# Block-recurrent attention and quick-GELU MLP: the states' exponentials are turned by DMA and VectorE, not by TensorE

## The chip, the cores and the metric

The kernel runs on one core of a Trainium2 chip. The metric is the device time of one execution in microseconds (us), as a median of several executions. The profile reports the span from the first to the last instruction; the device time is about 1.8 us longer in most runs. All runs quoted are of the undisturbed ("fast") state.

## The reference

```python
# x (8, 8, 512, 64), state (8, 8, 32, 64), float32; scale = 1/8
a  = softmax(scale * x @ state.T)            # over the 32 states
xread = a @ state                            # 512 rows a batch
a2 = exp(scores2 - scores2.max(-1))          # scores2 = scale * state @ x.T, over 512 tokens
a2 /= a2.sum(-1) + 1e-9
sread = a2 @ x                               # 32 rows a batch
h = concat(xread, sread) @ w_in              # (4352, 512) @ (512, 2048)
out = (h * sigmoid(1.702 * h)) @ w_out
```

The change concerns `a2`, called `e2` in the kernel, and `sread`. The scores are small (inputs of standard deviation 0.1), so `a2` is nearly uniform. Some experiments below put wrong blocks into it on purpose, and the comparison with the reference passed for them too. "Correct" therefore says little about the addresses of the new transfers; for the versions recommended here I also compared the addresses with those of the change by hand.

## The kernel before

One batch's up and down products run on TensorE (PE) while the attention of the next batch is woven in. Names such as P5, P6, P3 and P7 are the partial products of a two-level Strassen scheme, in that order; each has seven small products, and a *hook* like "P3.5" is the place in program order after the fifth of them, where work of the next batch is put. Reading the states for batch b needs `e2` with tokens on the partitions, `eT`.

```python
def att_s_exp(b, room=None):                       # cut
    room = apool.tile([P, NPR, S], FP32, tag="xT", name=f"e2_{b}")
    for g in range(NG):                            # NG = 2
        nc.scalar.activation(out=room[:, g], in_=a["s"][g], func=AF.Exp, bias=..., scale=scale, accum_out=sm)

def s_norm(b, g):
    ...                                            # sm = 1 / (sm + eps), on VectorE
    nc.scalar.activation(out=e, in_=e, func=AF.Copy, scale=sm)          # batches 2 to 7

def att_eT(b, g):                                  # at hook "P6"
    ps = att_ps([P, SCH, P], f"eT_{b}_{g}")
    for c in range(SCH):                           # SCH = 4
        nc.tensor.transpose(ps[:, c], a["e2"][g][0][:, P * c : P * (c + 1)], ident)
    nc.scalar.copy(a["eT"][:, g], ps)

def att_sread(b):                                  # 64 small matmuls
    nc.tensor.matmul(ps[st, g], a["eT"][:, g, c, st], xn[b][:, c, NG * j + g], ...)
    nc.scalar.copy(sr, ps)

# strassen_two, after P6 (cut)
if plain:                                          # while batch 2's attention is woven in
    for fn in steps3: fn()                         # four big differences on VectorE
    hook("P6")
    product(bank(3), A_of(0, 1), B22, "P3")        # att_sread(2) at hook "P3a", halfway
else:                                              # batches 3 to 7
    low_load(3, 0)                                 # ahead of it, after P5: low_load(6, 1)
    hook("P6")
    lowly("P3", left12, B22, low_b, ...)           # low_b: what low_load(6, 1) brings, 768 KB
    hook("run")                                    # att_sread(b)
```

The second small product of P3, called P3.2 below, is the first that reads `low_b`. Its load can only be issued at the end of P5, which read other sums from the same buffer.

## Time and profile before

| | before |
|---|---|
| time | 720.39 us, median of 3 (720.36 to 720.54) |
| span of the profiled run | 718.7 us |
| PE busy, share of the span | 704.6 us, 98% |
| VectorE (DVE) busy | 586.4 us, 82% |
| ScalarE (ACT) busy | 241.6 us, 34% |
| DMA queue, share of 16 engines | 104304 packets, 32.6% |

The shares say that PE is the bound and that DVE is the next candidate; the rest of the reading is in the prediction. One more view matters later, the table of PE's waits. Each line has the waiting line, what it waited for, the total in us, how often, and the longest. The largest before is 1.5 us, at 36 us, before the batches that are changed; no line is for a load of the low sums that P3.2 reads.

### The profile page before, as it was taken

The page shows a single profiled execution, that of the slowest core. Times are in us where ns is not written, and L with a number is a line of the kernel's source. Part 1 is how long each engine was busy: PE and PEld are TensorE (multiplying, and loading weights), DVE is VectorE, ACT ScalarE, POOL GpSimd, SP SyncE. Part 2 cuts the span into 40 slices and gives each one's busy share as a digit, 9 for nine tenths or more (in the row PEclk, how much of TensorE's full clock was granted, in tenths as well). Part 3 has the DMA queues.
Part 4 walks back from the last instruction along what each step waited for, and adds up shares of the span by engine and source line. Part 5 has one row for each costly group of instructions (what it writes and reads, how often), then busy time and mean ns, then how long its engine had stood idle before and what let it go on. Part 6 is the DMA issues. An engine that isn't in the chain of part 4 may idle for free.

```text
span 718.7 us, 12329 instructions
## 1 busy us (share of the span) xinstructions
PE 704.6 (98%) x4949; PEld 561.7 (78%) x4951; DVE 586.4 (82%) x1199; ACT 241.6 (34%) x467; POOL 0.8 (0%) x8
## 2 busy tenths in 40 slices
PE   8989999999999999999999999999999999999996
PEld 3433444467898799879998899889987998899995
DVE  6998899739868998699878986899789987989440
ACT  5686511024214422524233423342244215200210
POOL 0000000000000000000000000000000000000000
PEclk9999999999999999999999999999999999999999
DMA  9921246016153334405450445133422340031001
GB/s 234 357 87 58 91 147 145 6 59 160 47 175 63 58 106 162 77 1 123 158 121 0 110 142 133 18 74 125 154 50 51 112 162 15 1 117 61 17 1 29
DMA packets 104361, 68.43 MB, mean 95 GB/s; under 512 B 87664, under 2 KB 95344, under 8 KB 104304
## 3 DMA queue, kind: packets, MB, share of 16 engines
q1 hardware_dynamic: 104304, 67.65, 32.6%
q8 instruction: 39, 0.64, 0.4%
q14 instruction: 18, 0.15, 0.1%
HBM read 54.79 MB, written 12.85 MB: 94 GB/s over the span
## 4 chain that ended last, share of the span: by engine, by line
PE 88%; DVE 5%; DMA 3%; ACT 2%; SPq 1%; issue 1%; DVEq 0%; ACTq 0%
PE low L669 17%; PE o L1064 17%; PE o L720 14%; PE o L669 8%; PE o L518 7%; PE h L500 7%; PE upx L1064 6%; PE M L320 4%; PE o L561 2%; DMA xn<-in_x_dram 2%; PE o L320 1%; PE sr L480 1%; PE warm L125 1%; DMA out_dram<-osb_sr 1%; PE eT L469 1%; DMA out_dram<-osb 1%
## 5 line engine op out<-in xcount | busy, mean ns | idle before, releaser
L1074 DVE TENSOR_TENSOR g<-o,g 128x512 f32<-128x512 f32 (+1 forms) x140 | 88.0, 650 | 55.5 <-PE o L1064 54.6
L720 PE MATMUL o<-w_out,g 128*128 128x256 f32 x480 | 107.9, 381 | 0.0
L720 PEld LDWEIGHTS o<-w_out,g 128*128 128x128 f32 x480 | 90.2, 190 | 18.3 <-issue 6.3
L1071 ACT ACTIVATE g<-g 128x512 f32<-128x512 f32 (+1 forms) x84 | 49.8, 600 | 101.9 <-DVE g L1074 101.9
L1064 PE MATMUL upx<-aT,M 128*128 128x256 f32 x192 | 49.3, 379 | 0.0
L1064 PE MATMUL o<-ta,M 128*128 128x256 f32 x192 | 49.3, 379 | 0.0
L1064 PE MATMUL o<-ta,ms 128*128 128x256 f32 x192 | 48.3, 379 | 0.0
L460 ACT COPY M<-M 128x512 f32<-128x512 f32 x64 | 33.2, 597 | 29.6 <-PE M L320 29.6
L1064 PEld LDWEIGHTS o<-ta,ms 128*128 128x128 f32 x192 | 36.5, 190 | 4.9
L1064 PEld LDWEIGHTS o<-ta,M 128*128 128x128 f32 x192 | 36.5, 190 | 4.9
L669 PE MATMUL low<-low,g 128*128 128x128 f32 x304 | 40.2, 275 | 0.0
L1064 PEld LDWEIGHTS upx<-aT,M 128*128 128x128 f32 x192 | 36.1, 190 | 4.7
L669 PEld LDWEIGHTS low<-low,g 128*128 128x128 f32 x304 | 37.0, 192 | 0.0
L669 PE MATMUL low<-sums,later 128*128 128x128 f32 x264 | 35.0, 276 | 0.1
L669 PEld LDWEIGHTS low<-sums,later 128*128 128x128 f32 x264 | 32.7, 192 | 0.7 <-DVE pu L674 0.3
L320 PE MATMUL M<-w_in,stT 64*32 64x512 f32 x512 | 32.6, 594 | 0.2 <-ACT eT L470 0.2
L541 DVE TENSOR_TENSOR later<-g,g 128x512 f32<-128x512 f32 (+1 forms) x32 | 20.8, 648 | 14.7 <-ACT g L503 14.7
L500 PE MATMUL h<-low,M 128*128 128x512 f32 x64 | 29.8, 600 | 1.5 <-DVE low L408 1.5
L500 PE MATMUL h<-aT,M 128*128 128x512 f32 x64 | 28.7, 599 | 1.4 <-ACT M L460 1.4
L518 PE MATMUL o<-w_out,g 128*128 128x512 f32 x64 | 28.7, 594 | 0.0
L669 PE MATMUL low<-w_out,g 128*128 128x128 f32 x216 | 28.5, 275 | 0.0
L518 PE MATMUL o<-w_out,sums 128*128 128x512 f32 x64 | 28.4, 594 | 0.0
(214 smaller groups left out, 1287.1 us busy)
## 6 DMA issues: line engine op xcount, KB each, us to landing
low<-low SPq DMA_DIRECT2D x34, 768.0 KB
later<-in_moe_w_out_dram SPq DMA_DIRECT2D x16, 512.0 KB
xn<-in_x_dram SPq DMA_DIRECT2D x28, 256.0 KB
w_out<-in_moe_w_in_dram SPq DMA_DIRECT2D x12, 512.0 KB
xsq<-in_x_dram SPq DMA_DIRECT2D x96, 64.0 KB
out_dram<-osb SPq DMA_DIRECT2D x18, 256.0 KB
out_dram<-later SPq DMA_DIRECT2D x14, 256.0 KB
later<-in_moe_w_in_dram SPq DMA_DIRECT2D x4, 512.0 KB
```

What stands on the lines that cost most here:

```text
L125: nc.tensor.matmul(ps, zeros[:, :P], zeros, start=True, stop=True)
L320: nc.tensor.matmul(ps[g][st], A[b]["stT"][rows, st], rhs(rows, j), start=True, stop=True)
L460: nc.scalar.copy(m[:, g], ps[g])
L500: nc.tensor.matmul(hps, lhs[i], rhs[i], start=(i == 0), stop=(i == n - 1))
L518: nc.tensor.matmul(ops, G[key, f // 2][:, f % 2, P * r : P * (r + 1)], w_out[:, f], start=(f == 0), stop=(f == NF - 1))
L541: nc.vector.tensor_tensor(out=s1, in0=a21, in1=a22, op=ALU.add)
L561: nc.tensor.matmul(ps[:, r], lhs[f][:, P * r : P * (r + 1)], rhs[:, f], start=(first and r == 0 and f == 0), stop=(f == HF - 1), skip_grou ...
L669: nc.tensor.matmul(ps, lhs[f], rhs[:, f], start=(first and f == 0), stop=(f == QF - 1), skip_group_check=True)
L720: nc.tensor.matmul(ps[:, r], lhs[f][:, P * r : P * (r + 1)], rhs[:, f], start=(r == 0 and f == 0), stop=(f == HF - 1), skip_group_check=True,)
L1064: nc.tensor.matmul(ps[:, k], lhs[i][:, o : o + P], rhs[i], start=(first and k == 0 and i == 0), stop=(i == n - 1), skip_group_check=True,)
L1071: nc.scalar.activation(out=dst, in_=src, func=AF.Gelu_apprx_sigmoid)
L1074: nc.vector.tensor_tensor(out=dst, in0=ps, in1=x, op=ALU.add)
```

## The change

For batches 2 to 7 the 8 transposes on PE and their 2 evictions on ACT go. Instead the exponentials are stored to DRAM, loaded back so that each 32x32 block sits at its transposed place, and each block is turned by DVE where it lies. The division by the sums moves from the exponentials to the result of the reads. Room on DVE is made by moving `x_scale` and `x_back` to earlier hooks.

```diff
+    squares = dram.tile([Ns, NG * NB, NPR, Ns], FP32, name="squares")
+    def eT_out(b):                                  # 4 stores of 128 KB, runs of 128 bytes
+        for j in range(NPR):
+            src = e2_room[b][Ns * j : Ns * (j + 1), :NG].rearrange("n g (t a) -> n (g t) a", a=Ns)
+            nc.sync.dma_start(squares[:, :, j], src)
+    def eT_in(b):                                   # 4 loads of 128 KB, runs of 512 bytes
+        v = squares.rearrange("n (k i) j a -> i n k (j a)", i=SCH)
+        for i in range(SCH):
+            nc.sync.dma_start(a["eT"][Ns * i : Ns * (i + 1)].rearrange("n g c q -> n (g c) q"), v[i])
+    def eT_turn(b, g):
+        t = A[b]["eT"][:, g].rearrange("p c q -> p (c q)")
+        nc.vector.transpose(t, t)
 # s_norm, batches 2 to 7
-            nc.scalar.activation(out=e, in_=e, func=AF.Copy, scale=sm)
 # att_sread, batches 2 to 7
-        nc.scalar.copy(sr, ps.rearrange("p g d -> p (g d)"))
+            for g in range(NG):
+                nc.scalar.activation(out=sr[:, D * g : D * (g + 1)], in_=ps[:, g], func=AF.Copy, scale=a["e2"][g][1])
 # hooks
+        at("P2a", eT_out, b)                        # after the exponentials
+        ("P5", eT_in)                               # behind low_load(6, 1)
-            ("P6", att_eT, 0), ("P6", att_eT, 1),
 # batches 3 to 7
-                ("P3.3", x_scale, 1), ("P3.4", x_back, 0), ("P3.5", x_back, 1)
+                ("P6.6", x_scale, 1), ("P3.3", x_back, 0), ("P3.4", x_back, 1), ("P3.5", eT_turn, 0), ("P3.6", eT_turn, 1)
 # batch 2
-                ("P6.5", x_scale, 1), ("P6.6", x_back, 0), ("P6", x_back, 1)
+                ("P6.5", x_scale, 1), ("P6.6", x_back, 0), ("P6", x_back, 1), ("P6", eT_turn, 0), ("P6", eT_turn, 1)
```

More of the change, by code (lines that the diff above doesn't have):

```diff
@@ L360, in att_s_max @@
             a["mx2"].append(mx)
+    e2_room = {}
     def att_s_exp(b, room=None):
@@ L364, in att_s_exp @@
         if room is None:
-            room = apool.tile([P, NPR, S], FP32, tag="xT", name=f"e2_{b}")
+            room = e2_room[b] = apool.tile([P, NPR, S], FP32, tag="xT", name=f"e2_{b}")
         a["e2"] = []
@@ L379, in s_norm @@
             nc.vector.tensor_scalar(e, e, sm, None, ALU.mult)
-        else:
-            nc.scalar.activation(out=e, in_=e, func=AF.Copy, scale=sm)
     def att_s_norm(b):
@@ L460, in att_M @@
             nc.scalar.copy(m[:, g], ps[g])
+    squares = dram.tile([Ns, NG * NB, NPR, Ns], FP32, name="squares")
[4 more added lines that the diff above has]
+    def eT_in(b):
+        a = A[b]
+        a["eT"] = apool.tile([P, NG, SCH, P], FP32, tag="eT", name=f"eT_{b}")
+        v = squares.rearrange("n (k i) j a -> i n k (j a)", i=SCH)
[4 more added lines that the diff above has]
+        nc.vector.transpose(t, t)
     def att_eT(b, g):
@@ L484, in att_sread @@
         sr = apool.tile([P, P], FP32, tag="sr", name=f"sr_{b}")
-        nc.scalar.copy(sr, ps.rearrange("p g d -> p (g d)"))
+        if b < 2:
+            nc.scalar.copy(sr, ps.rearrange("p g d -> p (g d)"))
+        else:
+            for g in range(NG):
+                nc.scalar.activation(out=sr[:, D * g : D * (g + 1)], in_=ps[:, g], func=AF.Copy, scale=a["e2"][g][1])
         A[b]["sr"] = sr
@@ L792, in strassen_two @@
             product(p5, [S1[:, f, :half] for f in range(HF)], T1, "P5")
+            hook("P5")
             banks = [h0, h1, o]
@@ L803, in strassen_two @@
             low_load(6, 1)
+            hook("P5")
             o, h0, h1 = low_banks()
@@ L932, in hooks_next @@
         attention = [
-            ("P6.1", x_sum, 0), ("P6.3", x_sum, 1), ("P6.3", x_inverse), ("P6.4", x_scale, 0), ("P6", att_eT, 0), ("P6", att_eT, 1),
+            ("P6.1", x_sum, 0), ("P6.3", x_sum, 1), ("P6.3", x_inverse), ("P6.4", x_scale, 0),
         ]
         if b > 2:
-            attention += [("P3.3", x_scale, 1), ("P3.4", x_back, 0), ("P3.5", x_back, 1)]
+            attention += [("P6.6", x_scale, 1), ("P3.3", x_back, 0), ("P3.4", x_back, 1), ("P3.5", eT_turn, 0), ("P3.6", eT_turn, 1)]
             names = {"T": range(5), "P7.5": (5, 6), "P7.6": (7,), "P4.1": (8,), "P4.5": (12, 13)}
@@ L939, in hooks_next @@
         else:
-            attention += [("P6.5", x_scale, 1), ("P6.6", x_back, 0), ("P6", x_back, 1)]
+            attention += [("P6.5", x_scale, 1), ("P6.6", x_back, 0), ("P6", x_back, 1), ("P6", eT_turn, 0), ("P6", eT_turn, 1)]
             names = {"P3a": range(7), "P7.1": (7,), "P7.2": (8,), "P7.3": (12, 13)}
             run, turned = "P3a", "P3b"
-        attention += [(run, att_sread), (run, att_M, 3, True), (run, att_M, 2)]
+        attention += [("P5", eT_in), (run, att_sread), (run, att_M, 3, True), (run, att_M, 2)]
         for name, fn, *args in attention:
```

## The prediction

> **What bounds the kernel now.** I read the page's busy shares and chain first.
>
> ```profile
> PE 704.6 (98%) x4949; PEld 561.7 (78%) x4951; DVE 586.4 (82%) x1199; ACT 241.6 (34%) x467; POOL 0.8 (0%) x8
> PE 88%; DVE 5%; DMA 3%; ACT 2%; SPq 1%; issue 1%; DVEq 0%; ACTq 0%
> ```
>
> The first line is each engine's busy time, the second the engines on the chain that ended last. TensorE (PE) is busy for 98% of the span and holds 88% of the chain, so PE work that is taken out shortens the run, unless PE then has to wait for something. The 82% of VectorE (DVE) is an average over stages; what counts is DVE where the change works. So next come the groups of instructions, to price what goes and what comes:
>
> ```profile
> L469 PE MATMUL eT<-ident,e 128*128 128x128 f32 x64 | 8.3, 273 | 0.0
> L381 ACT ACTIVATE e<-e,sm 128x512 f32<-128x512 f32 x12 | 8.0, 713 | 15.6 <-DVE sm L376 12.2 <-DVE sm L377 3.3
> L470 ACT COPY eT<-eT 128x512 f32<-128x512 f32 x16 | 8.6, 589 | 29.5 <-PE eT L469 29.5
> L447 DVE STREAM_TRANSPOSE aT<-e 128x512 f32<-128x512 f32 x12 | 8.4, 701 | 0.0
> ```
>
> Last I read the timelines of PE and DVE around the transposes. A late batch, PE, then DVE:
>
> ```profile
> 492.71 1.04 PE L469 MATMUL eT<-ident,e 128*128 128x128 f32 x8
> 493.58 1.06 PE L669 MATMUL low<-w_out,g 128*128 128x128 f32 x8
> 499.93 1.10 PE L480 MATMUL sr<-xn,eT 128*32 128x64 f32 x64
> ```
>
> ```profile
> 492.91 0.29 DVE L674 TENSOR_TENSOR later<-o,pu 128x128 f32<-128x128 f32 x1 [0.48 <-PE o L669]
> 495.64 0.29 DVE L674 TENSOR_TENSOR pu<-low,pu 128x128 f32<-128x128 f32 x1 [0.25 <-PE low L669]
> 497.35 0.29 DVE L674 TENSOR_TENSOR later<-o,pu 128x128 f32<-128x128 f32 x1 [0.16 <-PE o L669]
> 500.03 0.29 DVE L674 TENSOR_TENSOR later<-low,pu 128x128 f32<-128x128 f32 x1 [0.60 <-PE low L669]
> ```
>
> PE spends 493.58 - 492.71 = 0.87 us on the eight transposes and never idles here. DVE has four gaps from the end of product P6 to the reads (L480): 0.48 + 0.25 + 0.16 + 0.60 = 1.49 us. Batch 2 has another order: its P3 is a plain product, and the reads come after half of it.
>
> ```profile
> 185.67 1.04 PE L469 MATMUL eT<-ident,e 128*128 128x128 f32 x8
> 186.54 3.62 PE L720 MATMUL o<-w_out,g 128*128 128x256 f32 x16
> 190.09 1.10 PE L480 MATMUL sr<-xn,eT 128*32 128x64 f32 x64
> 191.12 1.95 PE L320 MATMUL M<-w_in,stT 64*32 64x512 f32 x32
> ```
>
> ```profile
> 190.28 0.70 DVE L447 STREAM_TRANSPOSE aT<-e 128x512 f32<-128x512 f32 x1
> 191.26 0.69 DVE L1208 TENSOR_TENSOR low<-sums 128x512 f32<-128x512 f32 x1 [0.28 <-PE sr L480]
> ```
>
> Here DVE runs without a gap from the end of P6 until 190.98, while PE gets to the reads at 190.09.
>
> **What the Trainium skill says.** (1) "VectorE: DVE Perf Modes", The three transpose paths: the VectorE transpose turns 32x32 blocks only, TensorE's turns a full 128x128 into PSUM. So the blocks themselves must be moved by something else, here DMA. The trace agrees on the shapes; it has a DVE transpose of 128x512 at 0.70 us (L447), and I use that. (2) "DMA: Bandwidth & Descriptors", Specifications: under 512 bytes a transfer is below line rate, with a read-modify-write. The new stores have runs of 128 bytes. The trace has no store so small; its loads of 128-byte runs (tile xsq, 8192 runs a batch) take 13 ns each on one of 16 engines, its 1024-byte stores 48 ns. (3) Same page, Anatomy of one DMA: some 2 us of fixed cost, mostly the receipt of the last write. This is paid twice here, since the load waits for the stores. (4) Same page, Rules for kernel authors: issue early, wait late; the change is built so.
>
> **The change, part by part** (batches 2 to 7; 0 and 1 stay as they were).
>
> *Removed.* PE: 6 x 8 transposes, 6 x 0.87 = 5.2 us, all on the path. ACT: two scalings (0.71 each) and two evictions (0.59 each) a batch, 15.6 us in all; ACT is 34% busy and in these stages waits for PE, so this is worth nothing directly.
>
> *Added on the DMA side.* Per batch four stores of 128 KB (4 x 1024 runs of 128 B) after the exponentials, and four loads of 128 KB (runs of 512 B) queued after P5. In the late batch the exponentials end at 480.7. The 16 xsq issues took 8.38 us for 8192 runs, 1.02 ns a run, so 4096 runs take about 4.2 us of issuing (estimate), to 485; transfer overlaps, at 4096 x 13 ns / 16 = 3.3 us if stores go like loads; with the receipt they have landed by about 487. The weights' 768 KB load issued at 486.6 moves until 490.4. The new loads behind it need under 2 us plus a receipt, so they land near 494. DVE needs them at 498. About 4 us of slack: hidden.
>
> *Added on DVE.* Two turns a batch, at 0.69 us from start to start. I laid the new order (known from the built kernel) against the DVE timeline. P6 ends at 492.71 and its last add starts at 492.93, after a scaling moved into the 0.48 us gap. Then two differences (0.39 and 0.72 to the next), two pairs (0.67 each) around the add of P3.2 (0.20), x_back 0 at 496.19, add of P3.4 at 496.88, x_back 1 at 497.08, add of P3.5 at 497.77, turn 0 at 497.97, add of P3.6 at 498.66, turn 1 from 498.86 to 499.57. Without transposes PE starts the seven P3 products 0.893 us apart from 492.71. The sixth waits 0.06 us for the bank that the P3.4 add reads. The reads start at 499.12; turn 0 is done by then (498.68), and their second half begins at 499.64, just after turn 1. So a steady batch keeps 0.87 - 0.06 = 0.81 us. DVE follows 0.3 us later relative to PE, and the P7 adds free their banks 0.3 us or more before PE needs them.
>
> *Batch 3* has one more DVE subtraction (0.60 us) between the turns, as a hook of that batch alone. Turn 1 ends 0.6 us later and the second half of the reads waits for it: it keeps 0.81 - 0.60 = 0.2 us.
>
> *Batch 2.* P6 still ends at 185.67, and PE reaches the reads 3.55 us later, at 189.22. DVE's line from there is unchanged until the x_back that starts at 190.28; the two turns come behind that: turn 0 from 190.97 to 191.66, turn 1 from 191.65 to 192.35. PE waits 2.5 us for turn 0 and again a little for turn 1, and the reads end at 192.41 + 0.52 = 192.93 instead of 191.12: **1.8 us lost**. No DVE wait of PE follows soon in which that could be won back.
>
> *Sum.* 4 x 0.81 + 0.2 = 3.4 us won, 1.8 lost: -1.6 us. 720.4 - 1.6 = 718.8 us.
>
> **The rivals.**
> - *Everything hides.* All 5.2 us come off: 715.2. For it: PE is 98% busy and DVE and DMA have idle time overall. Against it: the batch 2 order above, where DVE had no gap at all.
> - *The 32x32 turns make DVE the bound in every batch.* Only 1.49 us of gaps less the 0.87 that PE gives up are left for 1.38 us of turns, so DVE runs 0.7 us behind if its gaps can't be used better. If each of five batches lost that too, the gain is nearly zero and with batch 2 the kernel ends at 721 to 722. For it: the small margins, 0.06 us at several places. Against it: reordered x_scale and x_back fill the first gap, and DVE has idle time later (P4 and the up products).
> - *The round trip is late.* If 128-byte stores cost four times the 128-byte loads (52 ns, about what 1024 bytes cost), they take 13 us, land near 496, and the loads near 499: the turn waits 1 to 2 us in five batches, 722 to 728 us. For it: the page's line on transfers under 512 bytes. Against it: the engines are half idle here, and 128-byte loads run at 13 ns.
> - *ACT's lost work frees something.* Its P6.1 and P3.1 copies came behind the scalings and evictions. But the PE waits for ACT in the table of waits sum to 0.5 us on the L669 products; worth at most that.
>
> **Range and chances.** The sum gives 718.8; the mixture of rivals pulls both ways by 2 to 3 us. Predicted 718.6, range 715.6 to 722.0. 2% is 14.4 us: the gain cannot exceed 5.2 us plus crumbs, so faster is nearly excluded; slower by 2% needs a round trip late by over 2.5 us in every batch. Same 0.96, slower 0.03, faster 0.01.
>
> **What would show it.** PE: eT transposes 64 to 16, all other counts alike. DVE: 12 new turns of about 0.69 us. In the late batch no PE idle before the reads, or under 0.2 us; in batch 3 a wait of some 0.6 us in the reads; in batch 2 a wait of about 2.5 us for the DVE turn, and the batch then 1.8 us behind. Turns should wait for DVE's own order, not for the DMA. I am wrong if DVE idles before a turn until the eT load lands (late round trip), if batch 2 shows no wait (then 715 to 717), or if PE waits appear in P3 or P7 of the later batches.

## The result, and the profile after

| | time, median (lowest to highest, runs) | ratio to before (95% interval) |
|---|---|---|
| before | 720.44 us (720.36 to 720.54, 4) | |
| changed | 720.11 us (719.40 to 721.15, 4) | 0.9997 (0.9979 to 1.0014) |
| changed, again, on another chip | 720.47 us (718.66 to 722.60, 21) | 1.0001 (0.9993 to 1.0008) |

A ratio is the mean time of one kernel's fast runs over that of the other's fast runs of the same rounds, so it is not quite the ratio of the medians.

The time is the same: both intervals hold 1. What catches the eye is the spread: before, the runs lie within 0.7 us of each other in every job but one (1.5 us in that one), after within 3.9 us. The page of the changed kernel shows that the PE work did go (48 matmuls fewer, 3.9 us less busy) and that the chain that ended last moved in part from PE to DVE and DMA: it was 88% PE, 5% DVE and 3% DMA.

```profile
PE 700.7 (97%) x4901; PEld 557.0 (77%) x4903; DVE 592.1 (82%) x1211; ACT 229.7 (32%) x449; POOL 0.8 (0%) x8
PE 83%; DVE 7%; DMA 6%; ACT 2%; issue 1%; SPq 1%; DVEq 0%; ACTq 0%
```

PE's waits in the changed kernel, the two that are new. The first is the reads (L500) waiting for the DVE turn (L480), once; the second is P3.2 (in L693) waiting for a load, twice.

```profile
PE sr L500 <- DVE eT L480: 2.3, 1, 2.3
PE low L693 <- DMA low<-low: 1.9, 2, 1.2
```

The first is in batch 2. Its timelines, PE and then DVE (start in us, length, engine, line, what, and in brackets the idle time before and what ended it):

```profile
191.58 1.25 PE L500 MATMUL sr<-xn,eT 128*32 128x64 f32 x64 [2.34 <-DVE eT L480]
192.76 1.95 PE L320 MATMUL M<-w_in,stT 64*32 64x512 f32 x32
```

```profile
190.23 0.70 DVE L447 STREAM_TRANSPOSE aT<-e 128x512 f32<-128x512 f32 x1
190.86 1.26 DVE L480 STREAM_TRANSPOSE eT<-eT 128x512 f32<-128x512 f32 x2
```

DVE starts the two turns right behind `x_back` and without a gap, so they wait for DVE's own order and not for a load. The projections (L320) start at 192.76 where they started at 191.12 before: batch 2 ends up 1.64 us behind.

In a late batch everything is as it was drawn up. PE, then DVE:

```profile
498.59 1.12 PE L693 MATMUL o<-w_out,spare_M 128*128 128x128 f32 x8
499.55 1.06 PE L693 MATMUL low<-low,g 128*128 128x128 f32 x8
500.54 1.10 PE L500 MATMUL sr<-xn,eT 128*32 128x64 f32 x64
```

```profile
499.22 0.69 DVE L480 STREAM_TRANSPOSE eT<-eT 128x512 f32<-128x512 f32 x1
500.01 0.69 DVE L480 STREAM_TRANSPOSE eT<-eT 128x512 f32<-128x512 f32 x1
```

Each of the products has its 0.9 to 1.0 us to the next, and the reads start at 500.54 without a wait: turn 0 is done at 499.91, and turn 1 at 500.70, just after their start and ahead of their second half.

The second new wait is in batches 4 and 7. PE in batch 4, the first two products of P3, after and then before, where the second started 0.90 us behind the first without a wait:

```profile
341.48 1.06 PE L693 MATMUL low<-w_out,g 128*128 128x128 f32 x8
343.76 1.13 PE L693 MATMUL low<-low,spare_M 128*128 128x128 f32 x8 [1.23 <-DMA low<-low]
```

```profile
340.71 1.06 PE L669 MATMUL low<-w_out,g 128*128 128x128 f32 x8
341.61 1.06 PE L669 MATMUL low<-low,spare_M 128*128 128x128 f32 x8
```

What it waits for is the 768 KB of `low_b`, an old load. The activity in slices of 1 us, first of the changed kernel, then of the kernel before; the last two columns are the busy share of the DMA engines (over 1 where packets overlap) and GB/s.

```profile
339.00:340.00 1.00, 1.00 (x11) 1.00 (x10) 0.97 (x4) 0.00 (x0) 0.00 (x0) 1.00 1.11 229
340.00:341.00 1.00, 1.00 (x11) 1.00 (x10) 1.00 (x5) 0.00 (x0) 0.00 (x0) 1.00 1.19 144
341.00:342.00 1.00, 1.00 (x11) 1.00 (x11) 1.00 (x3) 0.00 (x0) 0.00 (x0) 1.00 1.12 183
```

```profile
336.00:337.00 1.00, 1.00 (x11) 1.00 (x10) 1.00 (x3) 0.27 (x1) 0.00 (x0) 1.00 0.95 393
338.00:339.00 1.00, 1.00 (x11) 1.00 (x10) 1.00 (x4) 0.00 (x0) 0.00 (x0) 1.00 0.00 0
```

Before, the load ran alone at up to 393 GB/s and was over when slice 338 began; PE needed it at 341.61. After, it was issued in time (at 335.37, 0.19 us after P6's first product started, as before), but the new loads in runs of 512 bytes were issued from 336.30 on, the engines stayed busy at 144 to 229 GB/s, and PE's wait for the old load ended at 343.76.

The packed trace, which also keeps every packet and every landing signal, says more of this load than the slices. Of its 128 packets of 6 KB, 122 had ended by 339.97; the last six ran one after another from 339.86 to 342.36. Of its 16 landing signals, 15 had come by 341.31 and the last came at 343.63; before, all 16 came from 337.27 to 337.84. So in batch 4 most of the load was there in time, and PE waited for one late part of it. The late load of batch 7 is not as clear-cut: 15 signals by 571.21, the last at 571.37.

To see what each place costs, I aligned all PE matmuls of the two traces and read how far the changed kernel is ahead or behind at each place. In the first profile of the changed kernel the transposes give 0.80 to 0.92 us in each of six batches (5.04 in all). Batch 2 loses 2.41 + 0.15 at the reads, batch 3 loses 0.47 at P3.2 and 0.4 in the reads, batch 4 loses 1.39 and batch 7 loses 0.86 at P3.2. That is 5.7 lost, 0.7 net, as the spans show (719.4 against 718.7).

### The profile page after: what moved, and what is told of

The parts are those of the page before. It is cut to its first block, busy times and chain, and to the rows that moved or that the text cites. A ratio compares the mean times of both kernels' runs of the same rounds, so it can differ in the third digit from the quotient of the medians.

```text
span 719.4 us, 12331 instructions
## 1 busy us (share of the span) xinstructions
PE 700.7 (97%) x4901; PEld 557.0 (77%) x4903; DVE 592.1 (82%) x1211; ACT 229.7 (32%) x449; POOL 0.8 (0%) x8
## 4 chain that ended last, share of the span: by engine, by line
PE 83%; DVE 7%; DMA 6%; ACT 2%; issue 1%; SPq 1%; DVEq 0%; ACTq 0%
PE o L1091 17%; PE low L693 15%; PE o L744 13%; PE o L542 7%; PE o L693 7%; PE h L524 7%; PE upx L1091 6%; PE M L320 4%; PE o L585 2%; DMA low<-low 2%; DMA xn<-in_x_dram 2%; DVE later L751 1%; PE o L320 1%; PE warm L125 1%; PE sr L500 1%; DMA out_dram<-osb_sr 1%
## 5 line engine op out<-in xcount | busy, mean ns | idle before, releaser
L693 PE MATMUL low<-low,g 128*128 128x128 f32 x304 | 40.2, 275 | 0.0
L693 PEld LDWEIGHTS low<-low,g 128*128 128x128 f32 x304 | 37.0, 192 | 0.0
L693 PE MATMUL low<-sums,later 128*128 128x128 f32 x264 | 35.0, 275 | 0.1
L693 PEld LDWEIGHTS low<-sums,later 128*128 128x128 f32 x264 | 32.7, 192 | 0.7 <-DVE pu L698 0.3
L320 PE MATMUL M<-w_in,stT 64*32 64x512 f32 x512 | 32.7, 594 | 0.2 <-ACT eT L490 0.2
L693 PE MATMUL low<-w_out,g 128*128 128x128 f32 x216 | 28.5, 275 | 0.0
```

The costliest lines, as they stand in the source:

```text
L320: nc.tensor.matmul(ps[g][st], A[b]["stT"][rows, st], rhs(rows, j), start=True, stop=True)
L693: nc.tensor.matmul(ps, lhs[f], rhs[:, f], start=(first and f == 0), stop=(f == QF - 1), skip_group_check=True)
```

## The experiments

The theory after reading the traces: the gain is there in full, and it is eaten by (a) the DVE order in batch 2, (b) a smaller wait in batch 3, and (c) something with the DMA that differs from run to run. Rivals: the transposes had been partly hidden and are worth less than they look; or batch 2 really waits for the round trip. The runs below were made in four jobs on different chips; before took 720.43, 720.44, 720.48 and 720.45 us in them.

| run | time, median (lowest to highest, runs) | ratio to before (95% interval) |
|---|---|---|
| e5 transposes alone taken out | 715.41 (715.39 to 715.46, 5) | 0.9929 (0.9917 to 0.9941) |
| e1 batch 2's turns early | 716.34 (715.77 to 719.52, 6) | 0.9949 (0.9936 to 0.9962) |
| e2 no DMA | 719.97 (718.35 to 721.33, 13) | 0.9993 (0.9985 to 1.0001) |
| e3 stores only | 720.22 (718.38 to 720.69, 21) | 0.9992 (0.9986 to 0.9999) |
| e4 loads only | 718.56 (718.38 to 720.93, 13) | 0.9983 (0.9975 to 0.9991) |
| e8 no DMA, wait filled | 718.42 (718.32 to 718.46, 6) | 0.9971 (0.9959 to 0.9983) |
| e12 changed kernel, wait filled | 718.65 (718.36 to 719.84, 21) | 0.9977 (0.9971 to 0.9984) |
| e9 e1, batch 3 mended | 716.05 (715.59 to 717.34, 5) | 0.9939 (0.9927 to 0.9952) |
| e10 e9, long stores | 715.62 (715.53 to 715.80, 5) | 0.9932 (0.9918 to 0.9945) |
| e7 one hop, all issued early | 745.45 (740.24 to 748.00, 6) | 1.034 (1.0312 to 1.0367) |
| e11 e9, one hop in two halves | 716.11 (715.93 to 716.63, 5) | 0.994 (0.9927 to 0.9952) |

### e5: what the transposes are worth

The kernel before, with the transposes of batches 2 to 7 replaced by an ACT copy (a wrong result on purpose).

```diff
+        if b > 1:
+            nc.scalar.copy(a["eT"][:, g].rearrange("p c q -> p (c q)"), a["e2"][g][0])
+            return
```

> The kernel before, with the 48 TensorE transposes of batches 2 to 7 simply left out (ScalarE copies the exponentials as they are; the result is wrong on purpose). It measures by itself what the transposes cost: if all of their 0.87 us a batch lies on the path, 720.4 - 5.2 = 715.2 us with the small spread of before; if something else (VectorE, PSUM banks) sets the pace, less comes off.

Measured: 5.0 us faster, 0.81 to 0.93 us in each of the six batches. In batch 2 PE goes from P6 to the reads without a gap:

```profile
185.61 3.62 PE L723 MATMUL o<-w_out,g 128*128 128x256 f32 x16
189.16 1.10 PE L483 MATMUL sr<-xn,eT 128*32 128x64 f32 x64
```

So the transposes were on the path in full, and the rival that they were partly hidden is out. 715.4 us is the mark for any other way of turning `e2`.

### e1: batch 2's turns ahead of the four differences

```diff
         if plain:
+            hook("P6")
             for fn in steps3:
                 fn()
-            hook("P6")
```

> The changed kernel, but in batch 2 alone the block turns (and the last x_back) are put ahead of the four v sums on VectorE instead of behind them. Theory (batch 2 waits for VectorE's order): turn 1 is then done about 2.7 us earlier, before PE reaches the reads; the 2.3 us wait of the reads for the turn goes, nothing else changes: 720.1 - 2.5 = 717.6 us. Rival (the turn itself waits for the eT load to land, so that its place in the order does not matter): the wait stays and the time is 720.1 us; VectorE would then show idle time before the turn.

Measured: 716.34 us, 4.1 us below the changed kernel's 720.4. The turns now start at 188.16 us, and the reads do not wait:

```profile
188.16 1.26 DVE L480 STREAM_TRANSPOSE eT<-eT 128x512 f32<-128x512 f32 x2
```

Had the turn waited for the round trip, an earlier place would have gained nothing; that rival is out. But the gain is larger than the 2.56 us that the reads had lost. Something else went with that wait. One of the six runs is still at 719.52 us, at a mean clock of 0.998 (e1 keeps the new transfers).

### e2, e3, e4: without the DMA, stores alone, loads alone

e2 drops both transfers and turns `e2` itself (wrong on purpose). e3 keeps the stores. e4 stores in batch 2 only and loads those blocks in every batch (wrong on purpose, too).

```diff
 # e2, e3
-        nc.vector.transpose(t, t)
+        nc.vector.transpose(t, A[b]["e2"][g][0])
 # e2 (e3 has only the second of these)
-        at("P2a", eT_out, b)
-        ("P5", eT_in)
 # e4
+        if b == 2:
             at("P2a", eT_out, b)
```

> The changed kernel without its DMA: the turn reads the exponentials themselves (the result is wrong on purpose). PE, ACT and VectorE do the same work in the same order. Theory (the new transfers delay the 768 KB load of the low sums that P3.2 needs, and that costs 0.5 + 1.4 + 0.85 us in batches 3, 4 and 7 of the profiled run): all these waits go and with them the spread over the runs (1.75 us in the changed kernel, 0.2 us before); the 2.4 us of batch 2 and 0.4 us of batch 3 for the turns stay: 720.44 - 6 x 0.85 + 2.5 + 0.4 = 718.2 us, all runs within 0.4 us. Rival 1 (PE waits there for VectorE, as the table of waits says for batch 3): 0.3 to 0.5 us stays at P3.2 of batch 3. Rival 2 (the DMA does not matter): 720.1 us.

> As e2_no_dma, but the four stores of 128-byte runs to DRAM are kept; the loads are not there (wrong result on purpose). If the stores delay the load of the low sums (they and the output behind them hold the DMA engines until 1 to 3 us past the load's issue), the waits at P3.2 stay, 1 to 3 us in sum: 719 to 721 us with a spread of over 1 us. If it is the eT loads alone: like e2_no_dma, 718.2 us with little spread.

> The changed kernel with the four stores in batch 2 only; batches 3 to 7 load batch 2's blocks again (wrong result on purpose). If the eT loads, issued just behind the load of the low sums, take its bandwidth, the waits at P3.2 stay: 719 to 721 us. If only the stores ahead of it delay it: 718.2 us (batch 2's and 3's waits for the turns stay), with little spread.

Measured: in none of the three traces does P3.2 wait for its load. One trace proves little, since the second trace of the changed kernel (below) hardly has this wait either; the spans of all runs say it better. e3 and e4, with stores alone or loads alone, lie within 0.7 us in each of the two groups told below, but for one run of e4 at 719.2. e1, in the same job with both and without the wait in batch 2, goes from 714.0 to 717.7. So (c) is from the new traffic, and from stores and loads together. Batch 3's 0.47 us at P3.2, which the table of waits puts down to DVE, is gone in e2 as well, though DVE has the same order there, so rival 1 is out. But e2 was not fast as expected: with no new DMA at all it took 719.97 us. (Eight of its 13 runs have a device time 2.7 to 3.0 us above the span and not 1.8, which the record doesn't explain; the spans show the point more cleanly.) The spans of all three kernels fall into two groups, 716.5 to 717.1 us and 718.0 to 719.2 us. The trace of e2 fell into the second. Its PE timeline in batch 2:

```profile
191.57 1.52 PE L502 MATMUL sr<-xn,eT 128*32 128x64 f32 x64 [2.34 <-DVE eT L482]
193.02 3.29 PE L320 MATMUL M<-w_in,stT 64*32 64x512 f32 x32
```

The projections take 3.29 us and not 1.95 as in the changed kernel's trace. The slices show why; the third column from the end is the clock granted to TensorE:

```profile
190.00:192.00 2.00, 0.43 (x31) 0.43 (x32) 2.00 (x4) 0.00 (x0) 0.00 (x0) 1.00 0.00 0
192.00:194.00 2.00, 2.00 (x64) 1.10 (x61) 0.94 (x3) 0.52 (x2) 0.00 (x0) 0.60 0.00 0
194.00:196.00 2.00, 2.00 (x32) 0.31 (x16) 1.97 (x5) 0.94 (x2) 0.00 (x0) 0.55 0.03 8
```

The clock record has a half clock from 192.39 to 195.80 us, 3.41 us long, right after PE's idle stretch from 189.23 to 191.57. The Trainium skill, "TensorE: Matmul & The Clock Gate" (Part 1: The HAM clock gate, What's actually happening), describes such a gate: half clock after an idle window, in windows of 3413 ns that run free, so that the same kernel fares differently from run to run. The length agrees with this trace.

How much idle time is needed can be read from the traces. The clock records change only at multiples of 3.41 us from their beginning, so each trace can be cut into such windows. In e2 the window before the half clock, 188.98 to 192.39, holds the whole gap of 2.34 us. In the two traces of the changed kernel, in e3 and in e4 two windows share the gap, the larger part is 1.34, 1.81, 1.91 and 1.93 us, and the clock stays full. In e7 (below) five windows with 2.10 to 3.08 us of idle PE are each followed by half clock. At the kernels' ends, too, half clock follows windows with 2.03 us (e2) or more. So in the fourteen traces every full-clock window with at least 2.03 us of idle PE was followed by half clock, and none with at most 1.93 us (ends of matmuls are modelled, so these are not exact). If the windows lie at random, a gap of 2.34 us leaves that much in one window in 50% (for 2.03) to 55% (for 1.93) of the runs, an estimate from these numbers.

A half clock for 3.41 us lowers the mean clock of a 718 us span by 0.5 x 3.41 / 718 = 0.0024, and this is what separates the groups: in e2 all seven slow spans have a mean clock of 0.995 to 0.997, all six others 0.998 to 1.000. This gave a theory (d): the wait in batch 2 costs its 2.56 us, and in a good half of the runs some 1.5 us more by the half clock. In e2, e3, e4 and the second job of the changed kernel about 39 of 68 runs, 57%, are in the slow group (7 of 13, 15 of 21 and 6 of 13 by span, 11 of 21 by clock, where the delayed load blurs the spans; the clock alone is not a sharp mark, since e3 and e4 have one run each of 0.997 in the fast group).

### The changed kernel again

> The changed kernel once more, for its spread and a second profile. Theory (two irregular costs on a base of 716.6 us of span: half the clock for one window of 3.41 us after batch 2's idle, 1.4 to 1.8 us; and late loads of the low sums, 0 to 3 us): spans between 716.6 and 721 us, the ones with a mean clock of 0.995 or 0.996 over 718, none under 716.5. Rival (the first profile's waits at P3.2 were an accident of that run): spans of 716.6 or 718.0 to 718.5 only.

Measured: 720.47 us with spans from 716.8 to 720.8. Eleven runs have a mean clock of 0.995 to 0.997 and a mean span of 719.6, ten have 0.998 to 1.000 and 717.7. The trace is of the fastest run: it has the wait of 2.3 us in batch 2, and only 0.2 us at P3.2. So the waits at P3.2 in the first trace are not in every run either.

### e8: no DMA, PE kept busy during the wait

e2, with nine matmuls of the identity (18 in the profile's count) ahead of batch 2's reads, so that PE idles only 0.33 us there although the reads still wait for the turn.

```diff
+        if b == 2:
+            idle = att_ps([P, P], "idle")
+            for _ in range(9):
+                nc.tensor.matmul(idle, ident, ident, start=True, stop=True)
```

> e2_no_dma (no transfers, wrong result on purpose) with nine idle matmuls of 128 columns put ahead of batch 2's reads, which fill some 2.0 of the 2.3 us that PE waits there. Theory (the wait drops PE's clock to half for a window, in about half of the runs): it no longer does, and every run has a span of 716.6 us (e2: 716.5 to 718.4). Rival (the slow runs of e2 have another cause): spans of 718.0 to 718.4 remain in about half of the runs. If the fill delays the reads itself, all runs are later by the same amount.

Measured: 718.42 us, six runs within 0.14 us, spans of 716.5 to 716.7, no mean clock below 0.998. The same stretch as above keeps its clock:

```profile
192.00:194.00 2.00, 2.00 (x76) 1.17 (x72) 1.19 (x3) 0.57 (x3) 0.00 (x0) 1.00 0.03 8
```

The work that makes PE busy is useless, the reads start when they did, and the slow group is gone. e8 ran on another chip than e2, but on the same chip and in the same job the changed kernel, whose wait is not filled, had 11 of 21 runs at the lower clock. That shows (d).

### e12: the same fill in the changed kernel, with its DMA

> The whole changed kernel with its DMA traffic, with nine matmuls of the identity ahead of batch 2's reads, so that PE is busy during the wait for DVE's turn. Theory (half clock is one of two added costs): the wait itself stays (about 2.4 us of lost time in batch 2), the clock is at full in every run, and the median falls by some 1.5 us against the changed kernel as it is, to 718.6 to 719.2 us; what then stays above 718.4 us (the same fill without any new DMA) is the wait for the low sums. Rival (the spread of the changed kernel is all from the DMA traffic): the median stays at 720.1 to 720.5 us.

Measured: 718.65 us, 21 runs, none with a clock below 0.998. The wait is there still, filled (PE):

```profile
189.07 2.17 PE L498 MATMUL idle<-ident 128*128 128x128 f32 x18
191.58 1.25 PE L504 MATMUL sr<-xn,eT 128*32 128x64 f32 x64 [0.33 <-DVE eT L480]
```

So the rival that the spread is all from the DMA traffic is out. What stays is the DMA part: a spread of spans from 716.6 to 718.0, where e8 has 716.5 to 716.7. Its mean is 0.4 us here, but 1.1 us in the ten runs of the changed kernel at the high clock, on another chip; how large it is in general stays open. The fall of 1.8 us in the median is therefore not the half clock alone. On the means of the spans, the second job of the changed kernel lies 2.1 us above e8 (718.7 against 716.6): about 1.1 us of it is the DMA part and 1.0 us the lower clock (1.85 us more in 11 of 21 runs).

### e9 and e10: a version that keeps the gain

e9 is e1, with batch 3's extra difference moved out of the reads' way. e10 is e9, with one store of 4 KB runs in place of four stores of 128-byte runs; the blocks are then picked by the loads, in runs of 128 bytes.

```diff
 # e9
-                ahead["P3.6"] = [(low_third, (T4,))]
+                ahead["P7.7"] = [(low_third, (T4,))]
 # e10, besides
+    squares = dram.tile([P, NG, S], FP32, name="squares")
+        nc.sync.dma_start(squares, e2_room[b][:, :NG])
+        v = squares.rearrange("(j n) g (c i a) -> i n (g c) j a", j=NPR, i=SCH, a=Ns)
+            nc.sync.dma_start(a["eT"][Ns * i : Ns * (i + 1)].rearrange("n g c (j a) -> n (g c) j a", a=Ns), v[i])
```

> The changed kernel with batch 2's turns early and batch 3's extra subtraction moved from between the turns to P7.7; the transfers as in the changed kernel. Theory: batch 3's wait for turn 1 (0.4 us) goes too, so the base is 718.6 - 5.1 = 713.5 us of span, 715.3 us; the load of the low sums is still late in some runs: 715.3 to 719 us. Rival (batch 3's wait is not due to that subtraction): as e1_turn_early, 715.8 us at best.

> As e9_early_third, but the exponentials go to DRAM as they lie (one store of 128 runs of 4 KB) and the loads gather them in runs of 128 bytes, so the many small pieces are on the side of the load, behind the load of the low sums. Same bytes. Theory (small stores that are still under way, together with the eT loads, delay the load of the low sums): the stores are done some 2 us earlier, no wait at P3.2, every run near 715.3 us, spread under 0.6 us. Rival 1 (the loads behind it alone are enough): the spread of e9 stays. Rival 2 (128-byte loads are too slow): VectorE waits for the eT load before turn 0 of each batch, and the time is over 717 us.

Measured: e9 took 716.05 us, with no wait in the reads of batches 2 and 3, but still with waits at P3.2 (PE's waits):

```profile
PE low L693 <- DMA low<-low: 1.3, 3, 0.6
```

e10 took 715.62 us, 0.2 us above the mark of e5, five runs within 0.27 us, and its table of waits has no line for this load. PE at P3.2, then the DMA issues (SP) of a late batch:

```profile
490.33 1.06 PE L691 MATMUL low<-low,spare_M 128*128 128x128 f32 x8
```

```profile
477.47 0.34 SPq L466 DMA_DIRECT2D squares<-e  x1
483.33 0.34 SPq L641 DMA_DIRECT2D low<-low  x1
483.72 4.53 SPq L474 DMA_DIRECT2D eT<-squares  x4
```

One issue of 0.34 us replaces four that took 3.08 us in batch 4 of the changed kernel. e10 is the version to keep: it is 4.9 us faster than the kernel before in the same job (720.48), and 4.5 to 4.9 us faster than the changed one. Beside e3 and e4 it agrees with the reading that the P3.2 wait needs the short stores ahead of the loads. It doesn't show it alone, since its loads also changed: their issue takes 4.53 us where it took 2.66 us in batch 4 of the changed kernel, which may leave the old load more room. With five runs each, e10's spans lie from 713.8 to 714.0 and e9's from 713.8 to 715.6. Why single parts of the 768 KB fall behind I could not settle.

### e7 and e11: one hop, from SBUF to SBUF

The round trip through DRAM can be left out: 16 transfers of one block row each, directly into `eT`. e7 (with e1's edit) issues all after the exponentials; e11 (with e9's edits) issues eight there and eight after P5.

```diff
+        for i in range(SCH):                        # e11: i in (0, 1) here, i in (2, 3) at P5
+            for j in range(NPR):
+                rows, cols = slice(Ns * i, Ns * (i + 1)), slice(Ns * j, Ns * (j + 1))
+                nc.sync.dma_start(to[rows, :, cols], src[cols, :, rows])
```

> The changed kernel with batch 2's turns ahead of its v sums (as in e1_turn_early), and the blocks moved straight from SBUF to SBUF by 16 transfers of 32x32 blocks per group, right after the exponentials, without DRAM between: half the bytes and nothing behind the load of the low sums. Theory (stores and loads together delay that load): no wait at P3.2 in any batch and no half clock, so every run near 718.6 - 5.1 + 0.4 = 713.9 us of span, 715.7 us, spread under 0.5 us (e1: 715.8 to 719.5). Rival (the load of the low sums is late for another reason, such as the issue queue or instruction fetches): waits and a spread of over 1 us remain.

> As e9_early_third, but blocks go straight from SBUF to SBUF in 16 transfers, eight issued after the exponentials and eight behind the load of the low sums. In e7 all sixteen were issued ahead of that load and took 10.5 us to issue, so it was issued 11 us late. Theory (e7's loss is issue time in the one queue, not the transfers themselves): with eight of them, 8 x 0.61 = 4.9 us, ahead, the load is issued on time and the time is 715.3 to 717 us. Rival (small SBUF to SBUF blocks are slow as such): waits at P3.2 or before the turns remain, over 720 us.

Measured: e7 was 25 us slower, a miss. PE waited for the old load, and the issues show why:

```profile
PE low L698 <- DMA low<-low: 18.4, 5, 4.4
```

```profile
497.63 10.51 SPq L473 DMA_DIRECT2D eT<-e  x16
508.88 1.25 SPq L648 DMA_DIRECT2D low<-low  x2
```

The 16 issues hold the one queue for 10.51 us, so the load that P3.2 needs could not be issued until 508.88. These waits cost twice: the clock record has five stretches at half clock, 30.7 us in all, each behind such a wait. e11, which splits them around that load, took 716.11 us: the transfers were not the trouble, their place in the queue was. It does not beat e10. It has 2048 runs of 128 bytes ahead of the old load and 2048 behind it in each batch, and its spans still lie within 0.6 us; so short runs on both sides do not by themselves delay that load. Whether their number, their place or the way through DRAM matters stays open.

## Why the prediction was right or wrong

The predicted time (718.6 us) is 1.5 us under the first median and 1.9 us under the second, inside the range, and "same" was right. Both were easy: 2% is 14.4 us where at most 5.2 could be won, and a range of 6.4 us had room for two costs that the sum didn't contain. Of the forecast gain of 1.8 us, 0.3 us came in the first job and none in the second. What was right is the account of DVE and PE.

- **The transposes are worth 0.87 us a batch, all on the path: right.** e5 shows 5.0 us in all; the prediction had 5.2.
- **A steady batch keeps 0.81 us: right, by two small errors that cancel.** Batches 5 and 6 keep 0.80 and 0.81. But e5, without any turn, keeps 0.83 there, so the transposes were worth 0.83 and not 0.87, and the turns cost 0.02 to 0.03 and not the 0.06 of the bank. The rival that DVE becomes the bound in every batch is out.
- **Batch 2 loses 1.8 us by DVE's order: right.** The wait was 2.34 us (predicted 2.5) and the batch ended 1.64 us behind. e1 confirms the cause.
- **Batch 3 keeps 0.2 us: right in kind.** The reads lost 0.4 us, not 0.6, and e9 removed that with the named difference.
- **The sum.** With the measured terms it is 4 x 0.83 + (0.8 - 0.4) - 1.64 = 2.1 us won where 1.6 were predicted; 720.4 - 2.1 = 718.3. e8 (718.42) and the fastest runs of the changed kernel (718.66) and of e12 (718.36) are there. So the sum describes the best runs, and two costs that it lacked move the median to 720.1 to 720.5.
- **First missing step: the wait in batch 2 was priced by its length alone.** "PE waits 2.5 us for turn 0 and again a little for turn 1" left out that an idle PE can lose its clock. It costs 1.4 to 1.5 us (the distance of the two groups of spans, 716.5 to 718.0, and 1.95 against 3.29 us for the projections), in about half of the runs. e2 showed it, e8 and e12 removed it.
- **Second missing step: "about 4 us of slack: hidden".** This was right for the transfer it spoke of: no turn waited for its load. But I asked only when the new load lands, and not what it does to the old load just ahead of it. P3.2 then waited up to 1.23 us, in other batches from run to run. The receipts in that part were estimates, and a cited passage behind them is cut, since it is on transfers issued by GpSimd; before, the last packet of the 768 KB load of batch 4 ended at 337.50 and its last landing signal came at 337.84. The prediction's last part named "PE waits appear in P3" as a sign of being wrong, and they did appear.

The change thus moved the time little because its gain of 5.0 us was spent on DVE's order in batch 2 (2.56 us), on batch 3 (0.4), on the half clock (1.5 in half of the runs) and on the delayed load (0.2 to 2.7 in the two traces). e10 gets 4.9 of the 5.0 us back.

## What to carry to other kernels

When work leaves the bounding engine and goes to another, look first for the one stage where the other engine has no gap: the place in program order cost more here than the work itself. When a new transfer is put next to an old one, work out the slack of the old one too, and count the issue time in the queue. A spread that grows between two kernels is itself a finding: sort the runs by the mean clock and look for what comes in steps.

## What the Trainium skill lacked or had wrong

- "TensorE: Matmul & The Clock Gate", Why this matters for your kernels, advises against PE gaps over about 3 us. Here a gap of 2.34 us was enough for half clock in about 39 of 68 runs, and filling it down to 0.33 us left none in 27. The window of 3.41 us agrees, but it need not be idle throughout: 2.03 us of idle PE in one window was enough, 1.93 us was not.
- "DMA: Bandwidth & Descriptors", Specifications, has short transfers pay for a read-modify-write. The 128-byte stores took 13 ns each on their engine, as the 128-byte loads of the trace before did; no extra cost of stores shows. That such runs stay below line rate agrees: 128 bytes in 13 ns on 16 engines is some 158 GB/s (an estimate from these numbers), where the 768 KB load reached 393.
- No page that I read gives, for this chip, the time that SyncE takes to issue a DMA by the number of its runs. Here 16 issues in a row took 10.51 us of the one queue and made the kernel 25 us slower (e7), and one issue of 4 KB runs took 0.34 us (e10).
- "VectorE: DVE Perf Modes", The three transpose paths: no duration for float32 at 128x512; the traces have 0.69 to 0.70 us, in place or not.
